# A scan and two expert layers on one core: order of the first loads, one warm-up product, earlier rounding of the second expert's first weights

## The chip, the core and the metric

One core of a Trainium2 chip runs the whole program. Times are device microseconds (us) of that core. TensorE (PE) multiplies, with its weight loads listed apart (PEld); VectorE (DVE), ScalarE (ACT) and GpSimd (POOL) do the elementwise work; SyncE (SP) issues nearly all transfers. Less time is better.

## The reference, cut to what matters

```python
# 1. a scan over 768 steps: 4 batches x 8 heads, head size 32, state size 16
y = (C B^T * exp(cum_i - cum_j) * causal) x  +  (C state) * exp(cum)     # per chunk of steps
state = decay * state + (B * exp(cum_last - cum))^T x
# 2. four experts over the 3072 tokens, model size 256, hidden size 1024
p = domain_probs / (domain_probs.sum(-1) + 1e-9)
out = sum_e p[:, e] * (relu(x @ w1[e]) @ w2[e])
# 3. a dense gated layer, hidden size 1536
result = silu(out @ w_gate) * (out @ w_val) @ w_out
```

## The kernel before, in words

**Tiles and order.** The scan works in 24 chunks q of 128 steps (6 per batch, 4 batches), on 128 partitions. Its output is the experts' input, token tile by token tile: tiles 0 and 1 have 256 tokens, three have 512. For each tile the first two experts run, 8 hidden blocks each; such a block, unit (e, t, f), has 6 hidden products (line 616) and, three units later, 6 output products (line 624). Every operand that meets a product is split in two: ScalarE rounds it (high part), and VectorE or GpSimd subtracts that from the original (low part). A 256-token unit takes 12 products of 256 columns.

**Banks.** The hidden results use three PSUM banks in turn, so the hidden products of unit n need the bank of unit n-3, free when VectorE has made that unit's low part `hl` (line 658). The tile `y` (two banks) has one buffer: the scan's first outputs, the state sums `ds` of chunks 0 and 1, then `direct_scores(2)` (line 230) use it one after the other. Chunks 0 and 1's `ds` are copied out by `a_keep` (line 557).

**Weights.** `expert_load(e, part)` (line 168) brings 512 KB; parts 0 and 2 are halves of w1, parts 1 and 3 of w2. `expert_split(e, part, engines)` rounds on ScalarE (line 158, 128x1024) and subtracts on the engines named, each taking an equal share (line 162). Part (0, 0) and (0, 1) are split by hand in `begin` with `split_parts` (lines 268 and 272).

**The beginning.** The order is written out by hand, engine by engine: first the loads (lines 1147 to 1156), the constants, three products of ones (line 1161), four products that write the causal mask into PSUM (line 198), and then `begin` (line 284): clip and logarithm of `a` (lines 287 to 291), cumulative sums by products with a triangle (line 286), sums into rows (line 205), scores of chunk 0 (line 221), exponentials of chunks 0 and 1 (lines 253 and 248), weighting (line 257), outputs (line 539), rounding of the outputs into `xh`, `xl` (lines 578, 584). `crow` (line 328) is stored to DRAM (line 329), and the decay rows L of the later chunks are loaded from there, spread over all partitions (line 412); GpSimd masks them (`a_causal`, line 419), ScalarE exponentiates them (line 426, four instructions for each half).

**The slots.** After `begin`, a list `todo` puts further steps between the units. Slot 2u is behind the hidden products of unit u, slot 2u+1 behind the output products that follow; `put(s, fn)` appends to a slot. Each engine executes what is issued to it in that order. In slot 4 stands the mask of chunk 2, in slots 6 and 8 its exponentials, in slot 10 its scores (line 221, tile `direct`), in slot 12 the mask of chunk 3, in slot 18 its scores. Slot 3 holds `head_constants` (lines 137 to 151), `mixture` (lines 359 to 366, the normalised domain probabilities) and their store (line 368); slot 5 the state sums (`adds`), the loads of (1, 1) to (1, 3) and the split of (0, 3); slot 6 `a_keep`; slot 7 `totals` (line 276, with a small exponential on ScalarE); slot 8 the split of (1, 0). From unit 4 of a tile on, SP loads the probabilities back (`pbc`, line 652) behind their store. `PAIRS` (line 1189) gives, for each pair of later chunks, when its preparing steps are placed.

Of the kernel before, what the change touches and what calls it, by code (L numbers as in the profile page):

```python
# [11 lines left out]
AF = mybir.ActivationFunctionType  # L12
# [12 lines left out]
def kernel(ctx: ExitStack, tc: tile.TileContext, nat_d, bc_d, bc0_d, a_d, probs, w1, w2, wg, wv, wo, out):  # L25
# [96 lines left out]
    def keep(t, src, pattern, base, cm, op=ALU.is_ge):  # L122
        nc.gpsimd.affine_select(out=t, in_=src, pattern=pattern, base=base, channel_multiplier=cm, compare_op=op, fill=0.0)

    def constants():
        nc.vector.memset(ones, 1.0)
        nc.vector.memset(lower, -1e4)
        keep(upto, ones, [[1, P]], 0, -1)
        keep(above, lower, [[-1, P]], 0, 1, ALU.is_gt)
        nc.vector.memset(headsel, 1.0)  # L130
        nc.vector.memset(spaced, 0.0)
        keep(upper, ones, [[1, P]], 0, -1)
        keep(pick, ones[:, :16].rearrange("p (g r) -> p g r", r=4), [[-32, 4], [-1, 4]], 0, 1, ALU.is_equal)
        keep(lower, ones, [[-1, P]], 0, 1, ALU.is_gt)


    def head_constants():
        keep(headsel, headsel, [[-N, H]], 0, 1)
        keep(headsel, headsel, [[N, H]], N - 1, -1)

        nc.vector.tensor_reduce(
            out=csel, in_=headsel.rearrange("p (a l k) -> p l k a", l=2, k=2), axis=AX.X, op=ALU.add
        )
        nc.vector.tensor_tensor(out=csgn, in0=csel[:, 1, :], in1=csel[:, 0, :], op=ALU.subtract)

        nc.vector.tensor_tensor(
            out=pairblk,
            in0=headsel[:, :NP].rearrange("p (g k) -> p g k", k=2).unsqueeze(3).to_broadcast([P, KD, 2, D]),
            in1=headsel[:, NP:].rearrange("p (g k) -> p g k", k=2).unsqueeze(3).to_broadcast([P, KD, 2, D]),
            op=ALU.add,  # L150
        )
# [48 lines left out]
    def first_rows(rows):  # L200

        for r in range(4):
            for g, ps in enumerate(rows):
                group = slice(32 * g, 32 * g + 32)
                nc.tensor.matmul(
                    ps[:, r * P:(r + 1) * P],
                    pick[group, g, r:r + 1].to_broadcast([32, P]),
                    sums[group],
                    start=False,
                    stop=True,  # L210
                    skip_group_check=True,
                )

    def first_scores(q):

        ps = first[q]
        r = Q[q]
        for j in range(4):
            for z in range(2):
                rows = slice(z * 2 * N, z * 2 * N + N)  # L220
                nc.tensor.matmul(  # L221
                    ps[z][:, j * P:(j + 1) * P],
                    r["B0"][rows, j, :],
                    r["C0"][rows, j, :],
                    start=(j == 0),
                    stop=True,
                    skip_group_check=True,
                )
# [21 lines left out]
    def first_direct(q, z, ps):  # L250
        L = Q[q]["L"][z]
        for h in range(4):
            nc.scalar.activation(out=L[:, h, :], in_=ps[:, h * P:(h + 1) * P], func=AF.Exp, bias=cols(cum, q)[:, 4 * z + h:4 * z + h + 1])
# [30 lines left out]
    def begin(rows):  # L284

        mm = lambda out, w, v, start=False: nc.tensor.matmul(out, w, v, start=start, stop=True, skip_group_check=True)
        nc.vector.tensor_scalar(out=la, in0=la, scalar1=1e-6, scalar2=1.0, op0=ALU.max, op1=ALU.min)
        n = NFIRST * H
        nc.scalar.activation(out=spaced[:, :, :4], in_=la[:, :n].rearrange("p (g r) -> p g r", r=4), func=AF.Ln)
        nc.scalar.activation(out=la, in_=la, func=AF.Ln)  # L290
        nc.scalar.activation(out=wj[:, :1], in_=la[:, :1], func=AF.Exp)
        pt = hidden_bank(512)
        mm(pt[:, :P], spaced.rearrange("p g r -> p (g r)"), upper, True)
        py = ps_s.tile([P, 512], F32, tag="s", name="pc")
        mm(py[:, :n], upper, la[:, :n], True)
        nc.vector.tensor_copy(sums, pt[:, :P])
        nc.vector.tensor_scalar(out=cum[:, :n], in0=py[:, :n], scalar1=-1.0, scalar2=None, op0=ALU.mult)
        first_rows(rows)
        first_scores(0)
        pr = pt[:GR, P:3 * P]  # L300
        for g in range(2):
            mm(pr[:, g * P:(g + 1) * P], la[:, g * GR:(g + 1) * GR], upper)
        mm(py[:, n:NR], upper, la[:, n:])
        mm(py[:, 320:], lower, la)
        first_direct(0, 0, rows[0])
        first_decay(0, 1, rows[1])
        first_decay(1, 0, rows[2])
        first_exp(0, 1)
        first_weights(0, 0)
        first_decay(1, 1, rows[3])  # L310
        first_exp(1, 0)
        first[1] = out_banks(512)
        first_scores(1)
        for _ in range(2):
            mm(pt[:, 3 * P:], ones, ones)
        high, low = split_parts(0, 0)
        high(0)
        first_exp(1, 1)
        high(1)
        first_weights(0, 1)  # L320
        y = ps_y.tile([P, 2, 512], F32, tag="y", name="y01")
        for q in range(2):
            a_place(q, y)
        Q[0]["yv"] = hidden_bank(512)[:, :KD * P].rearrange("p (k i) -> p k i", k=KD)
        Q[0]["y"] = [Q[0]["yv"][:, k, :] for k in range(KD)]
        a_heads(0, True)
        first_weights(1, 0)
        nc.scalar.activation(out=crow, in_=pr.rearrange("p (g i) -> p g i", g=2), func=AF.Copy)
        nc.sync.dma_start(out=crow_d.rearrange("(g r) i -> r g i", g=2), in_=crow)
        expert_load(0, 3, bacc[0])  # L330
        a_load(2)
        a_load_cum(2)
        expert_load(1, 0, bacc[4])
        a_load_nat(2)
        a_load_cum(3)
        a_load_nat(3)
        first_weights(1, 1)
        low(0, nc.gpsimd)
        a_done_high(0)
        low(1, nc.vector)  # L340
        a_done_low(0)
        a_heads(1, True)
        nc.scalar.activation(out=wj, in_=py[:, 320:], func=AF.Exp)
        a_done_high(1)
        a_done_low(1)
        nc.vector.tensor_scalar(out=cum[:, n:], in0=py[:, n:NR], scalar1=-1.0, scalar2=None, op0=ALU.mult)
        high, low = split_parts(0, 1)
        high()
        for q in range(2):
            a_weigh_b(q, nc.gpsimd)  # L350
        low(0, nc.vector)
        return py, lambda: low(1, nc.vector)
# [55 lines left out]
    def a_load_cum(q):  # L408
        r = Q[q]
        src = crow_d[q * H:(q + 1) * H, :]  # L410
        r["L"] = at2.tile([P, H, P], F32, tag="L", name="L", bufs=4)
        nc.sync.dma_start(out=r["L"], in_=src.unsqueeze(0).to_broadcast([P, H, P]))
        if q >= NB:
            r["ec"] = at2.tile([P, P], F32, tag="ec", name="ec", bufs=4)
            nc.sync.dma_start(out=r["ec"], in_=src.unsqueeze(1).to_broadcast([H, N, P]))
# [270 lines left out]
    def high(out, raw):  # L686
        nc.scalar.activation(out=out, in_=raw, func=AF.Copy)  # L687
# [457 lines left out]

    with tc.manual_schedule():
        nc.sync.dma_start(out=la, in_=a_d)
        for q in range(NFIRST):
            a_load(q)
            Q[q]["L"] = [hpool.tile([P, 4, P], F32, tag=("hh", "hl")[q], name="L", bufs=(HB, LAG + 1)[q]) for _ in range(2)]  # L1150
        expert_load(0, 0)
        for q in range(NFIRST):
            a_load_nat(q)
        expert_load(0, 1)
        expert_load(0, 2, bacc[1])
        nc.sync.dma_start(out=pin, in_=probs)
        constants()
        s0 = ps_y.tile([P, 2, 512], F32, tag="y", name="s0")
        first[0] = [s0[:, z] for z in range(2)]
        for _ in range(3):  # L1160
            nc.tensor.matmul(first[0][0][:, :P], ones, ones, start=True, stop=True)
        rows = out_banks(512) + [hidden_bank(512) for _ in range(2)]
        for v in rows:
# [22 lines left out]
            return n0 + (i * NQE + j) * 4 + h  # L1186


        PAIRS = [(7.5, 1.2, 26), (9, 1.2, 46), (7, 1.3, 60), (6.3, 1.1, 72.5), (6.8, 0.9, 85), (4.3, 1, 95), (4.3, 0.8, 103), (5.8, 1, 117), (5.8, 1.1, 129), (6.8, 1.1, 141), (4.3, 1, 151)]

        def pair_loads(q):
            if q < NQ:
# [35 lines left out]
                expert_load(1, part, bacc[2 + (part + 2) % 4])  # L1228

        put(1, lambda: low_part())  # L1230
        put(3, lambda: (head_constants(), mixture(), mixture_store()))
        put(1, lambda: expert_split(0, 2, nc.vector))
        put(5, lambda: (adds(), loads()))
        put(6, keeps)
# [1 line left out]
        put(5, lambda: expert_split(0, 3, nc.vector))  # L1236
        put(11, lambda: pair_loads(4))

        for part, slot, engines in ((0, 8, (nc.vector,)), (1, 14, (nc.vector, nc.gpsimd,)), (2, 18, (nc.gpsimd,)), (3, 21, (nc.vector,))):
            put(slot, lambda part=part, engines=engines: expert_split(1, part, *engines))  # L1240

        seq, t1 = expert_tokens(0, bacc[4], bacc[5])
# [161 lines left out]
```

## Time and profile before

| | |
|---|---|
| median of 3 runs | 833.80 us (833.76 to 834.35) |
| the profiled execution | 834.19 us |
| its span, first to last instruction | 832.4 us |
| PE busy / PEld busy | 822.5 us (99%) / 683.7 us (82%) |
| DVE / ACT / POOL busy | 539.0 / 488.4 / 444.6 us |

The profiled execution's own time is 1.8 us over its span. The profile is that one execution; the runs' median is 0.4 us below it. Times in the rows below are from the start of the span. In a row of the timeline the text in square brackets is how long the engine sat idle before it, and what released it; `xN` counts merged instructions (an fp32 product counts twice).

### The profile page before, as it was taken

Reading aid. Unit: us, or ns where it says so; the run is one execution under the profiler, and the core shown is the slowest. Engines: PE = TensorE matmul, PEld = TensorE weight load, DVE = VectorE, ACT = ScalarE, POOL = GpSimd, SP = SyncE. Lnnn points to the kernel's source line nnn. Section 1 sums busy time; section 2 is a strip of 40 time slices with the busy share of each in tenths; the row PEclk is TensorE's granted clock in tenths of the full one; section 3 lists DMA queues with packets and bytes.
Section 4 is the critical chain, followed back from the end, with each engine's and each line's share of the span. In section 5 each row is a group of like instructions: output and inputs, shape, how many; then the busy total and the mean of one; then the engine's idle time right before and its main releaser. Section 6 shows DMA issues by size and latency. Waiting matters only on the chain.

```text
span 832.4 us, 12687 instructions
## 1 busy us (share of the span) xinstructions
PE 822.5 (99%) x4417; PEld 683.7 (82%) x4417; DVE 539.0 (65%) x830; ACT 488.4 (59%) x977; POOL 444.6 (53%) x448
## 2 busy tenths in 40 slices
PE   8999999999999999999999999999999999999997
PEld 7998888888778888888888888888888888888886
DVE  6777668565245946665657576648667676676675
ACT  6888777666465566667766666654444444444343
POOL 2665775434397424687785355406756358444351
PEclk9999999999999999999999999999999999999999
DMA  7875546551210153544323231763544365427301
GB/s 245 273 238 160 165 153 196 190 173 50 89 39 30 41 196 120 171 143 132 118 96 121 95 120 48 251 262 133 179 158 159 123 224 184 157 96 257 109 1 52
DMA packets 53296, 119.61 MB, mean 144 GB/s; under 512 B 5424, under 2 KB 19824, under 8 KB 53232
## 3 DMA queue, kind: packets, MB, share of 16 engines
q1 hardware_dynamic: 53088, 118.67, 42.3%
q8 instruction: 35, 0.57, 0.3%
q14 instruction: 29, 0.24, 0.1%
q10 hardware_dynamic: 144, 0.13, 0.0%
HBM read 101.34 MB, written 17.45 MB: 143 GB/s over the span
## 4 chain that ended last, share of the span: by engine, by line
PE 95%; ACT 2%; DVE 1%; issue 1%; ACTq 0%; DVEq 0%
PE h L936 30%; PE h L616 10%; PE d L1042 10%; PE po L1042 10%; PE po L624 10%; PE d L936 8%; PE po L1125 6%; PE d L1125 6%; PE scores L468 1%; PE ypsum L539 1%; PE ypsum L484 1%; DVE acc L679 0%; ACT we_h L687 0%; PE ypsum L497 0%; PE direct L221 0%
## 5 line engine op out<-in xcount | busy, mean ns | idle before, releaser
L1097 POOL TENSOR_TENSOR al<-s,ah 128x512 fp32r<-128x512 f32 x70 | 102.6, 1489 | 144.1 <-ACT ah L1095 112.2
L1095 ACT ACTIVATE ah<-s 128x512 fp32r<-128x512 f32 x72 | 45.3, 632 | 83.4 <-DVE s L1090 83.4
L1007 DVE TENSOR_TENSOR d<-d,c 128x512 f32<-128x512 f32 x32 | 22.4, 699 | 101.5 <-ACT c L1004 101.5
L658 DVE SCALAR_TENSOR_TENSOR hl<-h,hh 128x512 fp32r<-128x512 f32 (+1 forms) x80 | 46.3, 583 | 59.7 <-ACT hh L657 59.4
L991 DVE SCALAR_TENSOR_TENSOR hl<-h,hh 128x512 fp32r<-128x512 f32 x96 | 66.1, 689 | 20.6 <-PE d L1042 15.8
L1042 PE MATMUL po<-hh,we_o 128*128 128x512 f32 x256 | 78.9, 389 | 0.5 <-DVE acc L679 0.5
L1042 PE MATMUL d<-hh,we_o 128*128 128x512 f32 x256 | 78.8, 389 | 0.0
L990 ACT ACTIVATE hh<-h 128x512 fp32r<-128x512 f32 x96 | 57.1, 597 | 27.7 <-DVE h L1011 23.3
L657 ACT ACTIVATE hh<-h 128x512 fp32r<-128x512 f32 (+1 forms) x80 | 40.2, 509 | 52.8 <-PE h L616 52.4
L1085 ACT ACTIVATE s<-s 128x512 f32<-128x512 f32 x54 | 34.0, 632 | 45.5 <-DVE s L1084 44.7
L426 ACT ACTIVATE L<-L,cum 128x128 f32<-128x128 f32 x176 | 56.0, 394 | 4.8 <-POOL L L419 4.8
L616 PE MATMUL h<-xh,w_h 128*128 128x512 f32 (+1 forms) x160 | 56.7, 354 | 1.3 <-DVE hl L658 0.8
L624 PE MATMUL po<-hh,w_h 128*128 128x512 f32 (+1 forms) x160 | 56.4, 353 | 0.6 <-DVE tmp L677 0.6
L1042 PEld LDWEIGHTS po<-hh,we_o 128*128 128x128 f32 x256 | 48.0, 188 | 10.8 <-ACT we_o L687 0.9
L1042 PEld LDWEIGHTS d<-hh,we_o 128*128 128x128 f32 x256 | 48.1, 188 | 10.0
L936 PE MATMUL h<-xh,wq_h 128*128 128x512 f32 x144 | 56.1, 390 | 0.0
L936 PE MATMUL h<-xh,wq_l 128*128 128x512 f32 x144 | 56.0, 389 | 0.0
L936 PE MATMUL h<-xl,wq_h 128*128 128x512 f32 x144 | 56.0, 389 | 0.0
L616 PE MATMUL h<-xl,w_h 128*128 128x512 f32 (+1 forms) x160 | 55.6, 348 | 0.0
L624 PE MATMUL po<-hl,w_h 128*128 128x512 f32 (+1 forms) x160 | 55.5, 347 | 0.0
L616 PE MATMUL h<-xh,w_l 128*128 128x512 f32 (+1 forms) x160 | 55.5, 347 | 0.0
L624 PE MATMUL po<-hh,w_l 128*128 128x512 f32 (+1 forms) x160 | 55.4, 346 | 0.0
(244 smaller groups left out, 2385.0 us busy)
## 6 DMA issues: line engine op xcount, KB each, us to landing
wq_h<-wd_d SPq DMA_DIRECT2D x36, 448.0 KB
wq_l<-wd_d SPq DMA_DIRECT2D x36, 448.0 KB
L<-crow_d SPq DMA_DIRECT2D x22, 512.0 KB
bc<-in_bc_dram SPq DMA_DIRECT2D x21, 512.0 KB
wq_o<-wo_d SPq DMA_DIRECT2D x18, 512.0 KB
raw_q<-in_w_dram SPq DMA_DIRECT2D x32, 256.0 KB
pbc<-probs_d SPq DMA_DIRECT2D x22, 256.0 KB
wd_d<-wd_h SPq DMA_DIRECT2D x12, 448.0 KB
```

The costliest lines, as they stand in the source:

```text
L426: nc.scalar.activation(out=L[:, h, :], in_=L[:, h, :], func=AF.Exp, bias=cols(cum, q)[:, h:h + 1])
L616: nc.tensor.matmul(ps, w[:, k, fs], v[:, k, :], start=(i == 0), stop=(i == len(ops) - 1))
L624: nc.tensor.matmul(po[d], w[:, fc, dsl], x, start=(first and i == 0), stop=(last and i == 2))
L657: nc.scalar.activation(out=hh, in_=ph, func=AF.Relu)
L658: nc.vector.scalar_tensor_tensor(out=hl, in0=ph, scalar=0.0, in1=hh.bitcast(F32), op0=ALU.max, op1=ALU.subtract)
L936: nc.tensor.matmul(ps, x[:, ws], y, start=(start and i == 0), stop=(i == 2), skip_group_check=True)
L990: S.activation(out=hh, in_=ps, func=AF.Relu)
L991: return lambda: V.scalar_tensor_tensor(out=hl, in0=ps, scalar=0.0, in1=hh.bitcast(F32), op0=ALU.max, op1=ALU.subtract)
L1042: nc.tensor.matmul(po[d], both[:, z, dsl], y, start=(first and i == 0), stop=(last and i == 2), skip_group_check=True)
L1095: nc.scalar.activation(out=ah, in_=av, func=AF.Copy)
L1097: low.tensor_tensor(out=al, in0=av, in1=ah.bitcast(F32), op=ALU.subtract)
L1125: nc.tensor.matmul(po[d][:, z:z + n], x[:, dsl], y[:, z:z + n], start=(first and i == 0), stop=(last and i == 2), skip_group_check=True)
```

## The change

It reorders the first loads, drops two of three products of ones, rounds part (0, 0) in one piece ahead of the first exponentials and leaves both halves of its low part to GpSimd, moves `crow` ahead of the last exponential of `begin`, computes the head constants earlier, moves the mixture from slot 3 to slot 7, loads (0, 3) with the first loads and (1, 0) ahead of the decay rows of chunk 2, splits (1, 0) in slot 5 on VectorE and GpSimd and (1, 1) in slot 12, and changes one number of `PAIRS`.

```diff
@@ constants() / head_constants()
         keep(lower, ones, [[-1, P]], 0, 1, ALU.is_gt)
-
-
-    def head_constants():
         keep(headsel, headsel, [[-N, H]], 0, 1)
         keep(headsel, headsel, [[N, H]], N - 1, -1)
+
+
+    def head_constants():
@@ begin(rows)
         first_rows(rows)
+        head_constants()
         first_scores(0)
...
         mm(py[:, 320:], lower, la)
+        high, low = split_parts(0, 0)
+        high()
+        low(0, nc.gpsimd)
+        low(1, nc.gpsimd)
         first_direct(0, 0, rows[0])
...
         first_scores(1)
+        nc.scalar.activation(out=crow, in_=pr.rearrange("p (g i) -> p g i", g=2), func=AF.Copy)
+        nc.sync.dma_start(out=crow_d.rearrange("(g r) i -> r g i", g=2), in_=crow)
         for _ in range(2):
             mm(pt[:, 3 * P:], ones, ones)
-        high, low = split_parts(0, 0)
-        high(0)
         first_exp(1, 1)
-        high(1)
         first_weights(0, 1)
...
         first_weights(1, 0)
-        nc.scalar.activation(out=crow, in_=pr.rearrange("p (g i) -> p g i", g=2), func=AF.Copy)
-        nc.sync.dma_start(out=crow_d.rearrange("(g r) i -> r g i", g=2), in_=crow)
-        expert_load(0, 3, bacc[0])
         a_load(2)
+        expert_load(1, 0, bacc[4])
         a_load_cum(2)
-        expert_load(1, 0, bacc[4])
         a_load_nat(2)
...
         first_weights(1, 1)
-        low(0, nc.gpsimd)
         a_done_high(0)
-        low(1, nc.vector)
         a_done_low(0)
@@ the first loads
         nc.sync.dma_start(out=la, in_=a_d)
+        expert_load(0, 0)
         for q in range(NFIRST):
             a_load(q)
+            if q == 0:
+                nc.sync.dma_start(out=pin, in_=probs)
...
-        expert_load(0, 0)
         for q in range(NFIRST):
             a_load_nat(q)
         expert_load(0, 1)
         expert_load(0, 2, bacc[1])
-        nc.sync.dma_start(out=pin, in_=probs)
+        expert_load(0, 3, bacc[0])
         constants()
...
-        for _ in range(3):
+        for _ in range(1):
             nc.tensor.matmul(first[0][0][:, :P], ones, ones, start=True, stop=True)
@@ the tenth entry of PAIRS, and the slots
-(6.8, 1.1, 141)
+(6.3, 1.1, 141)
-        put(3, lambda: (head_constants(), mixture(), mixture_store()))
+        put(7, lambda: (mixture(), mixture_store()))
...
-        for part, slot, engines in ((0, 8, (nc.vector,)), (1, 14, (nc.vector, nc.gpsimd,)), (2, 18, (nc.gpsimd,)), (3, 21, (nc.vector,))):
+        for part, slot, engines in ((0, 5, (nc.vector, nc.gpsimd,)), (1, 12, (nc.vector, nc.gpsimd,)), (2, 18, (nc.gpsimd,)), (3, 21, (nc.vector,))):
             put(slot, lambda part=part, engines=engines: expert_split(1, part, *engines))
```

## Rows read from the trace of the kernel before

**Rows 1.** Timeline of PE, its three waits after the first hidden product: start us, us, instruction.
```profile
20.84 1.16 PE L221 MATMUL direct<-bc 16*128 16x128 f32 x16 [0.80 <-PE h L616]
...
26.55 0.39 PE L616 MATMUL h<-xh,w_h 128*128 128x256 f32 x1 [0.78 <-DVE hl L658]
...
47.23 0.36 PE L624 MATMUL po<-hh,w_h 128*128 128x256 f32 x1 [0.56 <-DVE tmp L677]
```
**Rows 2.** Windows: stretch, length, busy us of PE, PEld, DVE, ACT, POOL; clock; DMA share; GB/s.
```profile
60.00:832.00 772.00, 766.52 (x3836) 632.27 (x3834) 495.94 (x740) 442.58 (x860) 415.78 (x407) 1.00 0.40 135
2.00:10.00 8.00, 7.76 (x78) 6.36 (x79) 3.23 (x8) 4.74 (x13) 0.35 (x2) 1.00 0.95 320
```
**Rows 3.** Timeline of PE up to the first hidden product, same columns.
```profile
1.12 1.65 PE L1161 MATMUL s<-ones 128*128 128x128 f32 x6 [1.12 <-DVE ones L126]
4.26 0.63 PE L286 MATMUL h<-upper,spaced 128*128 128x128 f32 x2
...
5.37 0.58 PE L205 MATMUL po<-sums,pick 32*128 32x128 f32 x2 [0.23 <-DVE cum L297]
...
7.21 1.07 PE L221 MATMUL s<-acc 16*128 16x128 f32 x16
...
10.53 0.71 PE L286 MATMUL h<-ones 128*128 128x128 f32 x4
...
12.97 0.39 PE L616 MATMUL h<-xh,w_h 128*128 128x256 f32 x1 [0.50 <-ACT xh L578]
```
**Rows 4.** Timeline of ACT, same columns.
```profile
3.13 0.22 ACT L289 ACTIVATE spaced<-la 128x16 f32<-128x16 f32 x1 [1.05 <-DVE la L287]
...
5.05 0.20 ACT L291 ACTIVATE wj<-la 128x1 f32<-128x1 f32 x1
...
16.30 1.06 ACT L158 ACTIVATE w_h<-acc 128x1024 fp32r<-128x1024 f32 x1 [0.21 <-DMA acc<-in_w_dram]
...
21.12 1.28 ACT L426 ACTIVATE L<-L,cum 128x128 f32<-128x128 f32 x4 [3.49 <-POOL L L419]
...
23.86 1.04 ACT L158 ACTIVATE w_h<-acc 128x1024 fp32r<-128x1024 f32 x1
```
**Rows 5.** Timeline of DVE, same columns.
```profile
10.70 1.29 DVE L257 TENSOR_TENSOR L<-po,L 128x512 f32<-128x512 f32 x2 [0.17 <-PE po L221]
11.91 0.68 DVE L272 TENSOR_TENSOR w_l<-raw,w_h 128x512 fp32r<-128x512 f32 x1
...
17.05 0.15 DVE L141 TENSOR_REDUCE csel<-headsel 128x4 f32<-128x8 f32 x1
...
17.52 0.25 DVE L360 TENSOR_REDUCE psm<-pin 128x24 f32<-128x96 f32 x1
...
18.35 0.32 DVE L363 TENSOR_TENSOR pn<-pin,psm 128x96 f32<-128x96 f32 x1
...
18.92 1.22 DVE L162 TENSOR_TENSOR w_l<-acc,w_h 128x1024 fp32r<-128x1024 f32 x1
20.06 0.42 DVE L658 SCALAR_TENSOR_TENSOR hl<-h,hh 128x256 fp32r<-128x256 f32 x1
20.39 0.35 DVE L557 COPY st<-y 128x64 f32<-128x64 f32 x2
...
21.43 0.35 DVE L281 TENSOR_REDUCE dec<-totm 128x24 f32<-128x192 f32 x1
```
**Rows 6.** Timeline of POOL: two masks, a half of a split; DVE's half beside it.
```profile
19.78 1.31 POOL L419 TENSOR_SCALAR_AFFINE_SELECT L<-L 128x1024 f32<-128x1024 f32 x1 [6.05 <-DMA L<-crow_d]
...
27.91 1.29 POOL L162 TENSOR_TENSOR w_l<-acc,w_h 128x512 fp32r<-128x512 f32 x1 [3.64 <-ACT w_h L158]
...
28.20 1.55 DVE L162 TENSOR_TENSOR w_l<-acc,w_h 128x512 fp32r<-128x512 f32 x1
...
32.92 1.10 POOL L419 TENSOR_SCALAR_AFFINE_SELECT L<-L 128x1024 f32<-128x1024 f32 x1
```
**Rows 7.** Timeline of SP: the store from which later loads read.
```profile
11.69 0.34 SPq L329 DMA_DIRECT2D crow_d<-crow  x1
```

More of the change, by code (lines that the diff above doesn't have):

```diff
@@ L1186, in quad @@
             return n0 + (i * NQE + j) * 4 + h
-        PAIRS = [(7.5, 1.2, 26), (9, 1.2, 46), (7, 1.3, 60), (6.3, 1.1, 72.5), (6.8, 0.9, 85), (4.3, 1, 95), (4.3, 0.8, 103), (5.8, 1, 117), (5.8, 1.1, 129), (6.8, 1.1, 141), (4.3, 1, 151)]
+        PAIRS = [(7.5, 1.2, 26), (9, 1.2, 46), (7, 1.3, 60), (6.3, 1.1, 72.5), (6.8, 0.9, 85), (4.3, 1, 95), (4.3, 0.8, 103), (5.8, 1, 117), (5.8, 1.1, 129), (6.3, 1.1, 141), (4.3, 1, 151)]
         def pair_loads(q):
```

## The prediction, on record before the result

> **What bounds the kernel now.** I read TensorE's idle time first: after the first hidden product its timeline shows three waits, 0.80 us at 20.84 for the tile `y` (charged to a product, though the copies that free it had just ended), 0.78 at 26.55 for a low part `hl`, 0.56 at 47.23 for `tmp` [rows 1]. Then the windows: from 60 us on it is busy 766.5 of 772.0 us [rows 2]. So nothing after 60 us can give much, and the change, which works in the first 27 us, can give the start (first hidden product at 12.97) and the first two waits. Last I followed each engine's timeline backwards from those three places.
>
> The start: the first hidden product waits for `xh`, that for the outputs of chunk 1, those for VectorE's two weightings from 10.70, which waited for the scores of chunk 1 [rows 3, 5]. Up to there TensorE is the chain: ones from 1.12, the masks, the cumulative sum at 4.26, the row sums at 5.37, scores from 7.21 [rows 3].
>
> The two waits: the copies that free `y` stand at 20.39 in VectorE's queue, end at 20.74, and the instructions ahead of them follow each other without a gap [rows 5]. ScalarE meanwhile stands still for 3.49 us before the exponentials at 21.12, because GpSimd got chunk 2's decay rows only at 19.78 [rows 4, 6]. The split of (1, 0) comes behind them, at 23.86, and the `hl` that the second wait is for comes behind that.
>
> **The change, part by part**, in the clock of before; the gain of the start is subtracted at the end.
>
> *Two products of ones less.* They take 1.65/3 = 0.55 us each, 1.10 together. But the cumulative sum needs the logarithm, ready at 3.35 [rows 4], and its weights are loaded behind that; the masks, which end at 4.26, would end at 3.16 at the earliest. So the sum starts between 3.4 (right behind the logarithm) and 3.85 (with a whole load of weights, as long as the product, behind it); I take 3.65: 0.6 us earlier (0.4 to 0.85). Row sums then end at 6.6 instead of 7.21.
>
> *The clock.* A product of ones takes 0.55 us at 1.1 and 0.71/2 = 0.36 at 10.53 [rows 3]. The granted clock of the profile reads 1.00 all along, but the first duration is that of the lower level, 1.2 GHz, the second of 2.4. No row dates the rise; it lies between the two. I put it at the end of the row sums, 7.2, and keep that time: the 0.6 us by which scores begin earlier then run at half rate and give back 0.3. Ends: nothing given back, or all 0.6. **Start: 0.35 us gained** (0 to 0.7).
>
> *Rounding (0, 0) ahead of the exponentials; both low halves on GpSimd.* ScalarE is free from 5.25 [rows 4] to the row sums at 6.6, for 1.05 us of rounding (the 128x1024 row at 23.86), if the load has landed. `la`, this load and then chunk 0's operand are 1.15 MB; at 320 GB/s [rows 2] from about 2 us they are there at 4.0 and 5.6. This takes ScalarE's halves out from between the exponentials and 0.68 us from VectorE at 11.91 [rows 5], but neither is on the path of the start, which goes by the scores of chunk 1: gain nothing, cost nothing. GpSimd's 2 x 1.3 us are over by 9, used at 13. If the load came 1 us late, the exponentials would still end before VectorE's weightings.
>
> *Head constants and mixture.* The first three and the last four of seven instructions fill 17.05 to 18.67 [rows 5]. The constants (0.47) go into VectorE's gap before the row sums, the mixture (1.1) behind the copies: 1.55 us less ahead of them.
>
> *Loads.* (0, 3) goes into the queue with the first burst, so it no longer holds ScalarE at 16.30 (0.21) [rows 4]. The first burst is then 3.16 MB, done at about 11.9 by 320 GB/s. `crow`, issued some 2.4 us earlier than 11.69 [rows 7], waits behind that burst: 12.2; chunk 2's operands and (1, 0) then take 1.6 us each, to 15.4, the decay rows to about 17.1. GpSimd sees them at about 17.5, against 19.78. (1, 0) is seen at 15.8, its rounding needs it at 16.7.
>
> *Split (1, 0) in slot 5.* ScalarE does it from 16.95 to 18.0 in its idle time; the next `hh` is 0.6 us later than before, which VectorE, later still, does not feel. VectorE gets a half, 0.68 alone [rows 5], 0.61 net. Without more, the copies end at 20.74 - 1.55 + 0.61 = 19.80, TensorE is there at about 19.85, and the scores start 1.0 us earlier than 20.84.
>
> *But two engines want one path to SBUF.* Such a half took 1.55 us at 28.20 while GpSimd's half ran from 27.91 to 29.20: it started when that ended. The mask at 19.78, whose like takes 1.10 at 32.92, took 1.31 beside VectorE's split of 18.92 [rows 5, 6]. So a VectorE subtraction and a GpSimd instruction exclude each other. After the change VectorE's split of (0, 3) runs from 17.4 to 18.6 and the mask arrives within it, at 17.5 + 0.35 = 17.85. It takes the turn at 18.6 for 1.1 us, and VectorE's half of (1, 0) runs from 19.7 to 20.3. The copies end at 20.9, the scores start **0.1 us later** than before. If the mask comes behind 18.6 this costs nothing; if ahead of 17.4, GpSimd's own half comes between as well, another 0.9.
> The Trainium skill ("SBUF — State Buffer", section "Who interferes with whom") has a rule for this: VectorE with two SBUF inputs and GpSimd reading SBUF share a port pair, and one holds it for its whole instruction while the other is blocked. The trace agrees, 1.55 against 0.68. It speaks against this change: with the rule the first wait stays, without it the sum would be rival A's.
>
> *The second wait.* From the copies (20.9) VectorE does mixture 1.1, totals 1.1 (to 21.78 before, row 21.43 the last) and 0.4 behind GpSimd's state products: 23.5. Then ScalarE's small exponential and `hh` 0.5, `hl` 0.4: 24.4; exponentials of chunk 2, 1.28, `hh`, `hl`: 25.9. Before, the product began at 26.55 right behind its `hl`, so **0.65 us** come back in all by this point, the first wait's 0.1 included. With the port free, VectorE is 1.1 us earlier and TensorE, from 19.85 by 26.55 - 0.78 - 20.84 = 4.93 us of products, is there at 24.8: 1.75 in all.
>
> *The rest.* The store of the mixture now stands on SP behind three loads of 512 KB, landing at about 25; SP's `pbc`, and all loads for the next pair behind it, wait for that. Chunk 4's rows, a megabyte behind, then land some 4 us later, at 29 to 30; GpSimd masks them at 32.92 [rows 6], some 2 us earlier after the change: nothing, unless over a microsecond late. The wait at 47.23 stays: nothing in the change touches what it waits for. `PAIRS` moves steps by one slot where TensorE has no wait: nothing. (1, 1) in slot 12 has the same halves as before.
>
> **Sum:** 0.35 + 0.65 = 1.0 us off the profiled execution's 834.19, 833.2. That execution lies 0.4 above the median; I take the gain off the median: 833.8 - 1.0 = **832.8**.
>
> **Rivals.**
> A. *The port is free.* The decay rows come after 18.6: 1.1 us later than my sum of the transfers. Then 0.35 + 1.75 = 2.1: 831.7. For it: the second burst's start is not in any row. Against it: the 320 GB/s.
> B. *The load of (1, 0) is late (slower).* Its rounding now stands on ScalarE ahead of the fourth `hh`. Seen at time t, it is rounded at t + 1.05, then VectorE's half 0.61, `hl` 0.35, copies 0.35: the scores start at t + 2.4, and the second product follows 4.9 later. That passes 26.55 once t is over 19.3, and at 21.5 the kernel is 2.25 - 0.35 = 1.9 us slower, 835.7. Before, the load came fourth of its burst and was first used at 23.86, so no row says when it landed. Against: now it is second, behind 0.5 MB.
> C. *The clock rises later*, because TensorE has done less. If only at 10.6, the 4 us from 6.6 on give 2 us of work instead of 3.7: the start is 1.4 us later than before instead of 0.35 earlier, in all 834.5.
> D. *More than summed:* port free, early clock, the wait at 47.23 gone: 0.7 + 1.75 + 0.56 = 3.0, 830.8.
>
> **Chances.** Forecast 0.43, A 0.30, B 0.07, C 0.10, D 0.10. A measurement of this kernel tells about 0.2%, 1.7 us, from no change. Faster: A 0.25 (its lower end falls short), D 0.10, the forecast's better end 0.06: 0.41. Slower: B 0.07 and the far end of C 0.04: 0.11. Within: 0.48. The range leaves out B, half of D's and C's far ends: 830.7 to 834.6; the forecast's own is 832.1 (start 0.7, a little port wait) to 833.8 (the mask ahead of 17.4).
>
> **What would show it.** Row sums from about 4.8; the first hidden product at 12.6; GpSimd's first mask at 18 to 19 with VectorE's half behind it, over 1.2 us long from its issue; direct scores at about 20.6; the first product of the second expert at 25.5; the 0.56 us wait unchanged; loads for chunk 4 in time for GpSimd. Wrong would be: a VectorE half of 0.68 and copies by 19.5 (A), ScalarE idle before a split with a DMA as releaser (B), row sums at their old pace but scores over 1.5 us long (C).

## The result, and the profile after

Four runs each: the changed kernel takes 838.81 us (837.98 to 840.32), the kernel before 834.08 (833.76 to 834.43). The ratio is 1.0061, 95% interval [1.0049, 1.0073]: **4.7 us slower**, where 832.8 was forecast. The profiled execution took 838.17 us with a span of 836.4, 4.0 more than before.

TensorE's timeline of the kernel after (start us, us, instruction; in brackets the idle time ahead of it and what ended it) shows where the time came in:

```profile
1.12 0.80 PE L1162 MATMUL s<-ones 128*128 128x128 f32 x2 [1.12 <-DVE ones L126]
...
3.46 0.76 PE L286 MATMUL h<-upper,spaced 128*128 128x128 f32 x2
...
4.70 0.58 PE L205 MATMUL po<-sums,pick 32*128 32x128 f32 x2 [0.23 <-DVE cum L297]
...
6.54 1.96 PE L221 MATMUL s<-acc 16*128 16x128 f32 x16
...
10.75 2.08 PE L221 MATMUL po<-acc 16*128 16x128 f32 x16
12.75 1.22 PE L286 MATMUL h<-ones 128*128 128x128 f32 x4
...
16.34 0.58 PE L615 MATMUL h<-xh,w_h 128*128 128x256 f32 x1 [0.50 <-ACT xh L577]
...
17.40 0.41 PE L615 MATMUL h<-xh,w_l 128*128 128x256 f32 x1
17.61 0.34 PE L615 MATMUL h<-xl,w_h 128*128 128x256 f32 x1
17.79 0.28 PE L615 MATMUL h<-xh,w_h 128*128 128x256 f32 x1
...
21.85 0.39 PE L615 MATMUL h<-xh,w_h 128*128 128x256 f32 x1 [0.49 <-DVE hl L657]
...
25.52 1.16 PE L221 MATMUL direct<-bc 16*128 16x128 f32 x16 [1.25 <-issue]
...
29.30 0.39 PE L615 MATMUL h<-xh,w_h 128*128 128x256 f32 x1 [0.27 <-DVE hl L657]
```

Read it against [rows 1, 3]. The row sums start at 4.70 instead of 5.37 and the scores at 6.54 instead of 7.21: the head start is there. Then the same 16 score products take 1.96 us instead of 1.07, two products of ones 1.22 instead of 0.71, and the hidden products start about 0.21 us apart or more up to the one at 17.61, and from 17.79 on they are 0.12 apart. Those are the two levels of TensorE's clock, 1.2 and 2.4 GHz: in the kernel before the higher level was there when the scores started, here it came at about 17.6, and what TensorE does in between takes close to twice as long. The scores of chunk 1, 2.08 us at 10.75, take the same 2.08 in the profile of f2 below, where the granted clock does read 0.50. From the scores to the first hidden product it is 9.80 us (16.34 - 6.54) instead of 5.76, which with 0.67 of head start makes the first hidden product 3.37 us late. From there to the rise the first six of the hidden products take 1.45 us instead of 1.04. That is 3.8 of the 4.0 us by which the span grew.

The granted clock cannot be read from the windows here: this profile's first ones (length, busy us of PE, PEld, DVE, ACT, POOL, clock, DMA share, GB/s) say 1.00 all along:

```profile
0.00:13.00 13.00, 11.65 (x83) 9.33 (x84) 4.82 (x16) 7.44 (x14) 4.26 (x13) 1.00 0.87 281
...
60.00:832.00 772.00, 770.37 (x3871) 636.65 (x3870) 499.16 (x746) 446.08 (x871) 419.04 (x411) 1.00 0.40 136
```

What gives the clock away is the work done: 83 products in the first 13 us; the kernel before has 123 there. From 60 us on TensorE is busy 770.37 of 772 us, 3.9 more than in [rows 2]: that work came later, it did not grow.

The second thing to see is on VectorE and GpSimd. VectorE's timeline after:

```profile
19.36 2.10 DVE L162 TENSOR_TENSOR w_l<-acc,w_h 128x1024 fp32r<-128x1024 f32 x1
...
22.05 2.77 DVE L162 TENSOR_TENSOR w_l<-acc,w_h 128x1024 fp32r<-128x1024 f32 x2
...
25.08 0.34 DVE L556 COPY st<-y 128x64 f32<-128x64 f32 x2
```

and GpSimd's:

```profile
19.17 1.22 POOL L418 TENSOR_SCALAR_AFFINE_SELECT L<-L 128x1024 f32<-128x1024 f32 x1 [2.67 <-DMA L<-crow_d]
...
21.85 1.29 POOL L162 TENSOR_TENSOR w_l<-acc,w_h 128x512 fp32r<-128x512 f32 x1 [1.46 <-ACT w_h L158]
```

The subtraction that took 1.22 in [rows 5] takes 2.10 beside the mask, and the two merged ones at 22.05, a whole one and the half of slot 5, 2.77 beside GpSimd's half. The copies that free `y` end at 25.42 and the direct scores wait 1.25 us for them, where [rows 1] has 0.80. So of the two waits that the change works on, the first has grown. The second is gone from its product, the first one of the second expert (now at 30.83), but 0.49 at 21.85 and 0.27 at 29.30, for the `hl` of earlier units, are new: 2.0 us in all, where [rows 1] has 1.6 for the two. What was to come from here did not come.

### The profile page after: what moved, and what is told of

It reads as the page before. It is cut to its first block, busy times and chain, and to the rows that moved or that the text cites. A ratio compares the mean times of both kernels' runs of the same rounds, so it can differ in the third digit from the quotient of the medians.

```text
span 836.4 us, 12679 instructions
## 1 busy us (share of the span) xinstructions
PE 825.9 (99%) x4413; PEld 686.9 (82%) x4413; DVE 540.2 (65%) x829; ACT 488.4 (58%) x976; POOL 447.8 (54%) x450
## 4 chain that ended last, share of the span: by engine, by line
PE 94%; ACT 2%; DVE 2%; issue 1%; ACTq 0%; DVEq 0%
PE h L935 30%; PE h L615 10%; PE d L1041 10%; PE po L1041 10%; PE po L623 9%; PE d L935 8%; PE po L1124 6%; PE d L1124 6%; PE scores L467 1%; PE ypsum L538 1%; PE ypsum L483 1%; ACT hh L656 0%; DVE acc L678 0%; ACT we_h L686 0%; PE ypsum L496 0%
```

## The experiments

**Is it the two products of ones?** My theory after the result was that fewer products ahead of the scores put the rise off, and nothing else. The rival was that the new order of loads and rounding delays the beginning by itself. Both directions were run, and the value between.

e1, the change with three products:

```diff
-for _ in range(1):
+for _ in range(3):
```

> The changed kernel with three products of ones again, all else as changed. Clock theory (the loss is TensorE at its lower clock until 17.7 us, because the beginning gives it less to do): the half-rate products end near 7 us, the first hidden product comes at 12.5 to 13.1, and what is left is the gain summed behind the start, 0 to 1.2 us: 832.9 to 834.2. Order theory (the loss sits in the reordered loads and in VectorE's queue behind slot 5): 836.5 to 839, first hidden product still behind 15.

e2, the kernel before with one:

```diff
-for _ in range(3):
+for _ in range(1):
```

> The kernel before with one product of ones instead of three, all else as before. Clock theory: scores of chunk 0 take about 2.0 us instead of 1.1, first hidden product at 15 to 16.5, 836 to 838.5. Order theory: 833.3 to 834.5, no different from before, since the two products only fill time.

e3, the change with `range(2)`:

> The changed kernel with two products of ones. Clock theory: between e1 and the changed kernel; if the amount of work ahead of the masks decides it at a threshold, like one of the two (833 to 834.5, or 836.5 to 840), not halfway in each run. Order theory: as the changed kernel, 837 to 840.

| kernel | median us (lowest to highest, runs) | ratio to before, interval |
|---|---|---|
| before, run beside them | 833.68 (833.20 to 834.22, 19) | |
| e2 before, one product | 838.06 (837.66 to 838.65, 4) | 1.0052 [1.0037, 1.0067] |
| e1 change, three products | 834.00 (832.58 to 837.82, 10) | 1.0012 [0.9997, 1.0027] |
| e3 change, two products | 838.53 (836.77 to 839.85, 4) | 1.0050 [1.0033, 1.0067] |

Taking two products of 0.55 us out of the kernel before costs 4.4 us with nothing else touched; putting them back into the change returns 4.8. The rival falls: the loss comes without the new order, and with the new order it goes. e3 is like the kernel after, which both theories allowed. TensorE's timeline of e2 has the marks of the kernel after, and its products stay at half rate up to the one at 20.21:

```profile
6.58 1.95 PE L221 MATMUL s<-acc 16*128 16x128 f32 x16
...
16.38 0.58 PE L616 MATMUL h<-xh,w_h 128*128 128x256 f32 x1 [0.50 <-ACT xh L578]
```

and that of e1 those of the kernel before, without the first wait of [rows 1], and with 0.51 us for a `hl` one unit ahead of the second:

```profile
6.99 1.16 PE L221 MATMUL s<-acc 16*128 16x128 f32 x16
...
12.84 0.39 PE L615 MATMUL h<-xh,w_h 128*128 128x256 f32 x1 [0.50 <-ACT xh L577]
...
19.77 1.16 PE L221 MATMUL direct<-bc 16*128 16x128 f32 x16
...
23.76 0.39 PE L615 MATMUL h<-xh,w_h 128*128 128x256 f32 x1 [0.51 <-DVE hl L657]
```

e1's best run, the profiled one, is 832.58; but its ten spread over 5.2 us, where the kernel before stays within 1.0, and six of them lie outside the 832.9 to 834.2 that the clock theory gave. Two things were open: what makes it spread, and why the first wait was gone here.

**Slot 5 on VectorE alone.** e4 is e1 with the split of (1, 0) on `(nc.vector,)` instead of `(nc.vector, nc.gpsimd,)`, to see whether the shared split costs time.

> e1 with the whole low part of (1, 0) on VectorE, none of it on GpSimd. Port theory (VectorE's half waits a whole GpSimd instruction, as the 2.77 us of two subtractions in the changed kernel show): the two subtractions of slot 5 take 2.4 us (2 x 1.22) unless the mask of chunk 2 falls between, no worse than the halves; time equal to e1 or up to 0.6 us less. Rival (halving halves VectorE's work, no port): 0.6 us more than e1.

It took 834.72 (832.26 to 838.30, 10 runs), ratio 1.0021 [1.0004, 1.0037]; against e1 it tells nothing, since it spreads as widely. In its profile, of an execution of 837.68, the two subtractions of slot 5 take 2.35 us together, about the 2.4 of the port theory. TensorE's timeline there shows what a late run looks like:

```profile
6.98 1.43 PE L221 MATMUL s<-acc 16*128 16x128 f32 x16 [0.65 <-DMA acc<-in_bc_dram]
...
10.66 2.08 PE L221 MATMUL po<-acc 16*128 16x128 f32 x16
```

TensorE waits 0.65 us for the operand of chunk 0's scores, and the scores of chunk 1 behind that take 2.08, at the lower level. In the change that operand stands behind the load of (0, 0).

**The order of the first two loads.** f1 is e1 with the operand of the scores first; f2 is the kernel before with (0, 0) first and nothing else.

```diff
@@ f1, against e1
-expert_load(0, 0)
 for q in range(NFIRST):
     a_load(q)
     if q == 0:
+        expert_load(0, 0)
         nc.sync.dma_start(out=pin, in_=probs)
@@ f2, against before
 nc.sync.dma_start(out=la, in_=a_d)
+expert_load(0, 0)
 for q in range(NFIRST):
...
-expert_load(0, 0)
```

> e1 (changed kernel, three products of ones) with chunk 0's score operand loaded ahead of the weights of (0, 0), as in the kernel before. e1's ten runs went from 832.6 to 837.8; a profile with the same loads showed TensorE waiting 0.65 us for that operand between row sums and scores, and the rate falling to the lower level behind it. Theory (that wait is what makes the clock fall in some runs): no wait there, all runs 832.0 to 833.6. Rival (the spread comes from another part of the change): runs still reach over 836.

> The kernel before with the one load of (0, 0) moved ahead of chunk 0's score operand; three products of ones. Theory (the later operand makes the clock unsteady): a wait of 0.2 to 0.6 us before the scores, runs spread, some over 836. Rival (the load order does nothing by itself): 833.2 to 834.5 in all runs.

f1: 832.89 (832.35 to 836.50, 10 runs), ratio 0.9996 [0.9985, 1.0006]. f2: 834.41, ratio 1.0025 [1.0008, 1.0042], in two groups: six runs at 833.44 to 834.57 and four at 837.97 to 838.92. The profiled execution of f2 is one of the four. Its timeline of TensorE:

```profile
6.83 1.16 PE L221 MATMUL s<-acc 16*128 16x128 f32 x16 [0.36 <-DMA acc<-in_bc_dram]
...
10.17 2.08 PE L221 MATMUL po<-acc 16*128 16x128 f32 x16
```

and its windows (columns as above), in which the granted clock does show the fall:

```profile
4.00:8.00 4.00, 3.29 (x55) 2.83 (x54) 1.66 (x4) 2.70 (x8) 0.00 (x0) 1.00 1.00 352
8.00:15.00 7.00, 7.00 (x60) 5.82 (x60) 3.88 (x7) 3.21 (x8) 1.27 (x1) 0.50 0.33 110
15.00:21.00 6.00, 5.50 (x44) 4.84 (x37) 4.74 (x12) 4.03 (x8) 1.10 (x4) 0.50 0.89 275
21.00:26.00 5.00, 4.84 (x46) 4.67 (x45) 4.81 (x12) 2.04 (x6) 2.20 (x4) 0.93 1.04 358
```

0.50 from 8 to 21 us is the lower level, behind a wait of 0.36 us. The mean granted clock of each execution tells the same of the runs without a profile: in e1, e4 and f2 the ten runs over 837 us have 0.991 or 0.992, the other twenty 0.995 to 1.000. So the order of the first loads is a second cause, of the spread: with it alone four runs of ten come out at 838 to 839, without it none of the 27 of the kernel before is over 834.2. That the wait for the operand is what brings the fall is not shown. With the operand first, g1's profile (below) has as early a rise as f2's and a wait of 0.43 us behind it, and no fall; i1's has a wait of 0.54 us in the same place, and falls to 0.50 near 12 us. Their timelines of TensorE:

```profile
8.94 1.16 PE L221 MATMUL po<-acc 16*128 16x128 f32 x16 [0.43 <-ACT L L253]
```

```profile
9.20 1.16 PE L221 MATMUL po<-acc 16*128 16x128 f32 x16 [0.54 <-ACT L L253]
```

f1 has one run in ten at 836.50 all the same, and two more over the 833.6 that its theory allowed.

**The same number of products, later.** f3 is the change, f4 is e1, each with two products of ones behind the row sums, into a region that nothing reads. If the number of products were what counts, f3 would be as fast as e1.

```diff
 first_rows(rows)
+for _ in range(2):
+    mm(pt[:, 3 * P:], ones, ones)
```

> The changed kernel (one product of ones ahead of the masks) with two products of ones between the row sums and the scores of chunk 0, so the count is three again. If the amount of full-size products in the first 8 us decides the clock, wherever they stand: most runs 832.5 to 834.5, as e1. If it is what stands ahead of the row sums: 837 to 840, as the changed kernel, plus up to 1 us for the two products at half rate.

> e1 with two more products of ones in the gap between row sums and scores, where TensorE may wait for its operand anyway. Theory (idle or small products there make the clock fall): steadier than e1, all runs 832.5 to 834. Rival: spread as e1, 832.6 to 838.

f3: 840.04 (835.02 to 840.58, 6 runs), ratio 1.0066 [1.0046, 1.0085]; five of six are over 839: there the two products mostly do not help. The sixth, the profiled one at 835.02, has the higher level from about 9 us on (four products of line 286 take 0.68 us at 9.11, as in the kernel before, not the 1.17 of the kernel after), so where the products stand makes an early rise likely or unlikely and does not fix it. f4: 834.78 (833.04 to 835.83, 10 runs), ratio 1.0009 [1.0000, 1.0019]: no run over 836, but eight of ten over the 834 that its theory allowed. The two products lie on the path (the first hidden product comes at 13.21, in e1 at 12.84), and the profiled execution, 834.88, falls to a granted clock of 0.50 from 23 to 26 us.

**Who has the path to SBUF.** f1's profile has the case that the forecast had summed. VectorE's timeline of f1:

```profile
17.41 2.71 DVE L162 TENSOR_TENSOR w_l<-acc,w_h 128x1024 fp32r<-128x1024 f32 x2
...
20.37 0.34 DVE L556 COPY st<-y 128x64 f32<-128x64 f32 x2
```

GpSimd's:

```profile
18.44 1.13 POOL L418 TENSOR_SCALAR_AFFINE_SELECT L<-L 128x1024 f32<-128x1024 f32 x1 [5.09 <-DMA L<-crow_d]
```

In e1's profile the mask came at 18.73 instead, within the second of the two subtractions (1.82 together, from 17.25) and so behind both, and the copies stood at 19.32. VectorE's timeline and GpSimd's:

```profile
17.25 1.82 DVE L162 TENSOR_TENSOR w_l<-acc,w_h 128x1024 fp32r<-128x1024 f32 x2
...
19.32 0.35 DVE L556 COPY st<-y 128x64 f32<-128x64 f32 x2
```

```profile
18.73 1.29 POOL L418 TENSOR_SCALAR_AFFINE_SELECT L<-L 128x1024 f32<-128x1024 f32 x1 [5.53 <-DMA L<-crow_d]
```

0.3 us in the arrival of the mask make 1.05 us for the copies. That is what separates the forecast from rival A, and two kernels that differ only in the order of their first loads fall to either side. To take the collision out, g1 gives the split of slot 5 of f1 to GpSimd alone, g2 to VectorE alone; g3 is g1 with four products of ones.

```diff
-((0, 5, (nc.vector, nc.gpsimd,)), ...
+((0, 5, (nc.gpsimd,)), ...
```

> f1 (changed kernel, three products of ones, scores' operand first) with the whole low part of (1, 0) on GpSimd, behind the mask; VectorE has none of slot 5's second split. Port theory: the copies that free y no longer depend on when the mask comes, no wait before the direct scores (f1's profile had 1.04 us), 831.3 to 832.7, lower than f1's 832.9. Rival (the wait before the direct scores is not the port's): 832.3 to 833.5, as f1 or later, because GpSimd's 2.4 us come late for the first product of the second expert.

> f1 with the whole low part of (1, 0) on VectorE. Port theory: VectorE holds 1.22 instead of 0.68 us ahead of the copies, and still loses one mask's time when that falls in: 832.8 to 833.8, no better than f1. Rival (halving is what costs): better than f1 by 0.5 us or more.

> g1 with four products of ones. Clock theory: each product at half rate costs at most 0.55 us of the start and makes an early rise surer: median 831.8 to 833.2, and fewer runs (none of the ten or so) over 834.5. Rival (the late runs have nothing to do with the beginning's products): the same share of late runs as f1, 1 to 3 in ten, and 0.5 us more.

| kernel | median us (lowest to highest, 11 runs) | ratio to before, interval |
|---|---|---|
| g1 GpSimd alone | 833.80 (833.01 to 834.21) | 1.0000 [0.9991, 1.0008] |
| g2 VectorE alone | 833.49 (833.09 to 836.26) | 1.0002 [0.9993, 1.0011] |
| g3 GpSimd, four products | 833.41 (833.02 to 835.80) | 0.9999 [0.9990, 1.0007] |

None is to be told from before. g2's time is as expected; g1's lies over both of its ranges; g3 looks like its rival, 0.5 us over f1 with one late run in eleven. g1 has the copies early, at 18.86, and the direct scores without a wait at 19.68. The time goes elsewhere, in VectorE's timeline of g1:

```profile
20.34 2.07 DVE L362 TENSOR_TENSOR pn<-pin,psm 128x96 f32<-128x96 f32 x1
...
23.39 0.35 DVE L281 TENSOR_REDUCE dec<-totm 128x24 f32<-128x192 f32 x1
```

with GpSimd's beside it:

```profile
19.90 2.38 POOL L162 TENSOR_TENSOR w_l<-acc,w_h 128x1024 fp32r<-128x1024 f32 x1
```

and TensorE's next wait:

```profile
24.79 0.38 PE L615 MATMUL h<-xh,w_h 128*128 128x256 f32 x1 [1.61 <-DVE hl L657]
```

A product of 128x96 elements, 0.32 us in [rows 5], takes 2.07 and ends at 22.41, right behind GpSimd's subtraction, which ends at 22.28. Behind it stand `totals`, ScalarE's small exponential and `hh`, `hl`, so in place of the wait at `y` (0.80 before, 1.04 in f1) there is one of 1.61 at `hl`. The Trainium skill's rule ("SBUF — State Buffer", section "Who interferes with whom"), that VectorE with two SBUF inputs and GpSimd exclude each other for a whole instruction, agrees: 2.07 and, above, 2.10 and 2.77.

**Following the wait.** h1 is g1 with `totals` eight slots later, behind this stretch.

```diff
-put(7, lambda: totals(py[:, 320:]))
+put(15, lambda: totals(py[:, 320:]))
```

> g1 (changed kernel, three products of ones, scores' operand first, low part of (1, 0) on GpSimd) with totals in slot 15 instead of slot 7. In g1's profile the copies end at 19.2 and the direct scores need no wait, but the last step of the mixture (two SBUF inputs) takes 2.07 us beside GpSimd's split, totals follow it, ScalarE's small exponential waits for them ahead of hh, and TensorE waits 1.61 us. Port theory with that queue: hl of the fifth unit ends 1.2 us earlier or more, the 1.61 us wait is gone or under 0.5, 831.5 to 832.8 against 833.4 to 833.8 for g1 and before. Rival (something else holds TensorE there, such as the rounding or the exponentials of ScalarE): 833.0 to 834.0, as g1.

833.39 (832.29 to 833.94, 11 runs), ratio 0.9994 [0.9985, 1.0003]: over the 832.8 of the theory. Both waits are gone as it said, and a new one stands later in TensorE's timeline of h1:

```profile
19.27 1.16 PE L221 MATMUL direct<-bc 16*128 16x128 f32 x16
...
26.29 1.16 PE L221 MATMUL direct<-bc 16*128 16x128 f32 x16
...
31.52 0.36 PE L623 MATMUL po<-hh,w_h 128*128 128x256 f32 x1 [1.00 <-DVE acc L672]
```

followed back through VectorE:

```profile
30.95 0.76 DVE L672 TENSOR_TENSOR acc<-po,pbc 128x256 f32<-128x256 f32 x2 [0.66 <-DMA pbc<-probs_d]
```

to SP's queue:

```profile
21.96 0.37 SPq L367 DMA_DIRECT2D probs_d<-pn  x1
...
26.99 0.34 SPq L651 DMA_DIRECT2D pbc<-probs_d  x1
```

This is the store of the mixture and the load of the probabilities behind it, which the prediction saw stand behind three loads and costed at nothing. The direct scores of chunk 3 are 2.6 us earlier than before (26.29 against 28.91), and of those, 1.0 goes here.

i1 takes that out: h1 with `pin` loaded second, and the mixture and its store in the beginning, where the head constants are.

```diff
 head_constants()
+mixture()
+mixture_store()
 first_scores(0)
...
 nc.sync.dma_start(out=la, in_=a_d)
+nc.sync.dma_start(out=pin, in_=probs)
 for q in range(NFIRST):
...
-put(7, lambda: (mixture(), mixture_store()))
```

> h1 with the probabilities loaded second and the mixture computed and stored in VectorE's idle time ahead of the row sums' end, instead of slot 7. Store theory (h1's 1.00 us wait for acc is the store of the mixture standing behind three loads of 512 KB): that wait is gone, and the 2.07 us of VectorE beside GpSimd's split too; 831.3 to 832.8, 0.7 to 1.3 under h1's 833.4. Rival (pbc is late because all transfers are, whatever the store): a wait for acc remains, 833 to 834. If the mixture delays the exponentials of the beginning, up to 0.6 us is given back there.

832.74 (832.35 to 834.58, 11 runs; the kernel before, run beside it, 833.60, 15 runs), ratio 0.9990 [0.9981, 0.9999]: the fastest here, 0.9 us ahead of the kernel before. The profiled execution is its slowest, 834.58, with the clock at 0.50 from 12 to 18 us; in it the wait for the probabilities is gone, and the wait for `tmp` near 47 us is still 0.6.

## Why the prediction was wrong, point by point

**The clock: the step that failed.** The prediction put the rise "at the end of the row sums, 7.2" and then kept "that time". The date was right for the profiled execution of the kernel before, and a row that the prediction missed ("No row dates the rise") gives it; TensorE's timeline of before:

```profile
6.83 0.42 PE L205 MATMUL h<-sums,pick 32*128 32x128 f32 x2
7.00 0.39 PE L205 MATMUL po<-sums,pick 32*128 32x128 f32 x2
7.04 0.35 PE L205 MATMUL h<-sums,pick 32*128 32x128 f32 x2
7.21 0.29 PE L221 MATMUL s<-acc 16*128 16x128 f32 x2
```

The like products up to 6.83 take 0.42 us, the last one 0.35. What was wrong is to keep the date. It was treated as a point in time, though it hung on what TensorE did ahead of it, and the change takes away just that: two of three products of ones. Nor is it one date: with three products ahead, e1's profile has the rise near 6.2, and in e4's the first row sums take 0.38 us in place of 0.58, so it lies ahead of them. A line of e1, then one of e4:

```profile
6.35 0.27 PE L205 MATMUL h<-sums,pick 32*128 32x128 f32 x2
```

```profile
5.16 0.38 PE L205 MATMUL po<-sums,pick 32*128 32x128 f32 x2 [0.35 <-DVE csel L141]
```

Priced at 0.3 us given back, the loss of the two products costs 4.4 (e2). The bounds, nothing to all 0.6, came from the assumption and not from a row.

Rival C had the mechanism and the sign, but its price was one step too short: "if only at 10.6", where the trace has 17.6. 10.6 was the first row known to be at the higher level in the kernel before; with the two products gone nothing said that the rise would be there by then. With the rise behind the first hidden products, C would have read 833.8 + 3.4 + 0.4 = 837.6 us, and the range would have had to reach there.

**The start by fewer products.** Cumulative sum at 3.65 was summed, 3.46 measured; row sums 4.8, measured 4.70. Right within its bounds, and worth nothing at half rate. The 1.10 us summed for the two products themselves was too much: the masks start 0.82 earlier, at 1.74 instead of 2.56.

**Rounding (0, 0) in ScalarE's gap.** It ran from 5.13 for 1.06 us, ahead of the row sums' end: as summed. The loads, costed at nothing, were not: with (0, 0) ahead of the scores' operand that operand lands about when it is needed, at 6.83 in f2 and 6.98 in e4, and f2 has four late runs of ten. The prediction added up bytes to 5.6 us for this operand, 1 us ahead of its use, and weighed a late load only by the exponentials.

**The port.** Forecast: the mask arrives within the subtractions, copies at 20.9 less the start's 0.35. f1's profile has it so, 20.37; e1's has rival A, 19.32. Both occur; right in mechanism, and in the price of 1.1 us. The arrival was off: 17.85 was summed, and the mask came at 18.44 (f1), 18.73 (e1) and 18.84 (g1), at the edge of the 18.6 behind which rival A begins. In the kernel after, with all of TensorE's work later, the mask met the whole subtraction ahead instead, 2.10, and GpSimd's half came between as well: 2.77 against e1's 1.82, the other 0.9 that the prediction named for this case.

**The sum without the clock.** 0.65 us were summed behind the start. f1, which keeps the three products and mends the load order, came out 0.67 below before by the medians; its interval, -1.25 to +0.5 us, includes nothing gained. e1's best profile, with the port free, has a span 1.6 less than before, 0.13 of it at the first hidden product, against 1.75 summed behind the start for that case.

**Costed at nothing.** The mixture's store: covered as long as the rest is no faster; 1.0 us in h1. `PAIRS` and slot 12: no wait in the profile after that answers to them. The `tmp` wait stayed, 0.6. The slower rival B did not occur: ScalarE had (1, 0) before it needed it, and no split waits for a DMA.

## What to carry to other kernels

Products at the start that compute nothing may be holding up the clock for what follows: before taking any away, date the rise in the trace, of more than one execution, by durations of like instructions, and price the removal by everything behind them that could then run at the lower level, not by the products' own time. The order of the first loads belongs to the same question, since putting one load ahead of another made four runs of ten late (f2); repeat the run often enough to see two groups of times. And where two engines exclude each other, moving work between them moves the wait: follow it to the next name in the timeline before counting a gain.

## What the runs showed of the hardware

The size was not expected: two products of 0.55 us decide 4.4 us, and two do not do what three do (e3). Nor was it that their place matters beside their count: the same two behind the row sums left five of six runs of f3 over 839 us. With fewer than three ahead the date of the rise moved as well: 17.6 in the profile after, past 20.2 in e2's, about 20.9 in e3's.

Also unexpected is a fall in the middle of busy work. Besides f2 (0.36 us) and e4 (0.65 us), the profile of g3, an execution of 835.80 us, has a wait of 1.90 us and then this window:

```profile
26.00:30.00 4.00, 4.00 (x23) 4.00 (x22) 3.44 (x5) 4.00 (x13) 2.10 (x2) 0.57 0.58 116
```

TensorE is busy for all 4.00 us at a mean granted clock of 0.57. In other executions of the same kernel (833.02 at best) the mean over the run is 0.999 or 1.000, against 0.997 here. The profiles of e3 (near 28 us, behind a wait of 1.07), f4 (near 23, behind 1.04) and i1 (near 12) show such a fall too. The wait alone does not decide it: the kernel after waits 1.25 us, g1 1.61, f1 1.04 and h1 1.00, and the products behind those waits keep the higher rate.

The Trainium skill ("TensorE: Matmul & The Clock Gate", Part 1) says that the gate follows how busy the engine has been recently, that the point of the rise differs between runs of one kernel, and that the ramp costs below 1% of a typical span, so that a count of slow products should not be fitted. The second agrees: e1 and e4, the same kernel up to slot 5, rise near 6.2 and ahead of 5.2. So does the size: 4.7 of 834 us is 0.6%. On the first, the busy time of these profiles does not tell the level: f2 is busy 7.00 of 7.00 us at 0.50. And at this level of tuning 0.6% is more than all the rest of the change can give.

What exactly decides the rise and the fall stays open: the runs show that products ahead of the row sums make an early rise likelier, and a scores' operand in time a steady level, and not which property of the work the clock answers to. That the spread of e1 is due to the load order alone is not shown: with the operand first, f1 still has a run at 836.50 and g2 one at 836.26, both without a profile.
